# Moving one expert tile into the attention phase: units from pair 8, earlier routing, halved weight pieces, single scatter slots

## The chip, the cores and the metric

The kernel runs on one core of one Trainium2 chip. The metric is the device time of one execution in microseconds (us). Chips differ: in this study the kernel before took 203 to 210 us on two of them (12 and 4) and 221 to 226 us on two others (15 and 2). Every comparison below is a ratio to runs of the kernel before on the same chip. An execution over 1.5 per cent above the fastest of its kernel is called slow here; the ratios use the fast ones alone.

## The reference

Block-sparse attention (4 batches, 8 heads, 768 positions, head size 64) is followed by a mixture of experts in which each of the 3072 tokens goes to one of 8 experts.

```python
# attention: a window of +-15 positions, and 24 block summaries a head
k_sum = k.reshape(B, H, nb, 32, D).max(axis=3);  v_sum = v.reshape(B, H, nb, 32, D).mean(axis=3)
a = softmax([window scores | summary scores + log 32]);  x = a @ [v | v_sum]
# experts
logits = x @ w_gate + modality_bias[modality_id];  e_idx = argmax(logits, axis=1)
for e in range(8):
    mask = e_idx == e
    out[mask] = gate[mask, None] * (relu(x[mask] @ w1[e]) @ w2[e])
```

## The kernel before

Some words first. A **pair** is one of 16 attention steps (4 batches by 4 pairs of heads). After a batch's last pair its tokens are **routed** (steps on VectorE, taken by `tick`), and six indirect transfers, the **scatters**, write its rows to memory in the order of their experts. A **list** then names the tiles of 256 rows of one expert that are ready; `rows` loads them. An expert **tile** is cut into **units**: possibly a **turn** (the transposes `px` of its rows), four groups of the first product (`ph`), two of the second (`pmo`). `UNITS` says how many units run at each of six places of a pair; what attention does not take is left to the **tail**, behind attention.

```python
UNITS = {11: "111111", 12: "111111", 13: "111111", 14: "111111", 15: "101110"}   # 28 units
ENLIST = {9: 0, 12: 1, 15: 2}               # at the end of pair 9 comes batch 0's list, ...
# ...
def rows(lst, j, i):                        # cut: the last batch gathers by index instead
    row = nc.sync.value_load(lst["li"][0:1, j, 0:1], ...)
    nc.sync.dma_start(xr.bitcast(I32), xs[ds(row, 256)]...)
```

The weights of the two likeliest experts are loaded ahead, in pieces (`issue`, by the table `WAT`). Whether a tile's weight buffer really holds its expert is known only from the list. So each tile has a conditional reload of both products' weights that moves bytes only where the expert differs:

```python
def weights(lst, j, i):
    e = nc.gpsimd.value_load(li[0:1, j, 2:3], ...)
    go = nc.gpsimd.value_load(li[0:1, j, 3:4], min_val=0, max_val=1)
    load_weights(i % NWB, e, cond=go > 0)   # NWB = 2 buffers
# ...
def ahead():                                # called by enlist, by unit, and when the last piece is sent
    while todo and todo[0][2] < min(ended[0] + 1 + into[0] // 4, guessed[0]):
        lst, j, i = todo[0]; fetch(i); todo.popleft()
        weights(lst, j, i)
        pending.append(expert_tile(i))
# ...
WAT = {1: 1, 2: 1, 3: 1, 4: 2, 5: 1, 6: 2, 7: 2, 8: 2, 9: 2, 10: 2}   # quarters a pair; 8 are one expert
```

On this case's inputs no reload moves anything: the records of these instructions are 0.04 to 0.05 us long and have no packets. The loop over the pairs, cut to the places that matter (`pump` takes units, `scatter` one scatter from the queue unless told otherwise):

```python
for n in range(np_):
    scores(n, 0); ...; tick(1 if n < 10 else 2); pump(u[0]); blocks(n); ...
    scatter(early); pump(u[1]); ...; scores(n, 1); ...; scatter(early); pump(u[3])
    if n + 2 < np_: keys(n + 2); more(n + 2, (0, 1))
    ...; pump(u[4]); values(n, 0); scatter(); ...
    if n + 2 < np_: summaries(n + 2)        # GpSimd copies the block summaries into kv (line 276)
    issue(n)
    if u[3]: scatter(2)
    if n in ENLIST:
        scatter(len(scatters)); enlist(lists[ENLIST[n]])
    pump(u[5])
```

The softmax here doesn't subtract the row's maximum and nothing guards it: scores larger than these inputs give would overflow.

## Time and profile before

| | first profile | a cleaner repeat on chip 12 |
|---|---|---|
| this execution | 221.1 us | 203.9 us |
| span of the core | 219.2 us | 202.0 us |
| TensorE busy | 181.5 us | 174.6 us |
| granted clock, mean | 0.948 | 0.969 |
| timed runs | median 208.56 us (3 runs) | fast ones 203.84 and 205.82 us |

A timeline row gives start, duration, engine, line, operation, output<-input, and in brackets how long the engine had stood idle and what ended it. The first profile has 10.8 us of idle called "issue" in its second half; the repeat has none after 84 us. I use the repeat, a single execution, for comparisons. Here is its GpSimd timeline where the first reloads (line 233) and the second batch's scatters (line 372) are:

```profile
74.47 0.05 POOL L233 DMA_DIRECT2D w1b<-in_moe_w_dram  x1 [0.90 <-DMA w1b<-in_moe_w_dram]
74.92 0.04 POOL L233 DMA_DIRECT2D w2b<-in_moe_w_dram  x1 [0.40 <-DMA w2b<-in_moe_w_dram]
79.87 1.10 POOL L372 DMA_INDIRECT xs<-xb,posi  x1 [0.59 <-DVE ks L270]
...
87.95 0.04 POOL L233 DMA_DIRECT2D w2b<-in_moe_w_dram  x1 [1.42 <-DMA w2b<-in_moe_w_dram]
...
92.09 0.99 POOL L372 DMA_INDIRECT xs<-xb,posi  x1 [0.30 <-issue]
```

Tile 0's reload is met 0.9 and 0.4 us after GpSimd is free, tile 1's 1.42 us: the pieces that they must not overtake had almost all landed. The second batch's six scatters go out between 79.87 and 92.09.

### The profile page before, as it was taken

How to read it: one execution, taken by the hardware profiler on the slowest of the kernel's cores; microseconds unless marked ns; L12 is line 12 of the kernel's file. 1: busy time of each engine (PE TensorE's matmuls, PEld its weight loads, DVE VectorE, ACT ScalarE, POOL GpSimd, SP SyncE). 2: the span in 40 equal slices, each digit the busy share in tenths (PEclk: the TensorE clock that was granted, in tenths of full speed). 3: DMA queues.
4: the chain of work that ended last, by engine and by line, in shares of the span. 5: the costliest groups of instructions: out<-in, count | busy, mean ns of one | idle time of the engine just before them, and what ended most of it. 6: DMA issues, size and time to landing. Idle time of an engine off the chain costs nothing. (4 is left out here: it accounts for less than half of the span.)

```text
span 219.2 us, 7344 instructions
## 1 busy us (share of the span) xinstructions
PE 181.5 (83%) x3008; PEld 130.9 (60%) x3008; DVE 99.8 (46%) x335; ACT 129.4 (59%) x174; POOL 116.5 (53%) x189
## 2 busy tenths in 40 slices
PE   7679778798779669978999739999785999998860
PEld 2467667687669556655676524767362776676440
DVE  5378766866989993416348422353930000000000
ACT  2698779658886858757384223544433776575440
POOL 8786556556889539571303741206875337522540
PEclk9997999959979999999999966999999999999997
DMA  5999999998999999737200323203243222220220
GB/s 74 180 200 216 132 175 173 165 158 122 159 215 193 209 225 191 161 114 241 100 3 28 117 107 106 96 3 121 76 152 102 96 100 99 93 99 4 99 91 20
DMA packets 20141, 27.49 MB, mean 125 GB/s; under 512 B 2924, under 2 KB 16516, under 8 KB 20100
## 3 DMA queue, kind: packets, MB, share of 16 engines
q0 software_dynamic: 17472, 24.40, 54.1%
q1 hardware_dynamic: 2628, 2.54, 4.2%
q8 instruction: 26, 0.43, 0.8%
q14 instruction: 15, 0.12, 0.2%
HBM read 85.46 MB, written 10.17 MB: 436 GB/s over the span
## 5 line engine op out<-in xcount | busy, mean ns | idle before, releaser
L563 PE MATMUL ph<-xg,w1b 128*128 128x256 f16 x384 | 46.9, 273 | 4.2 <-issue 2.6
L575 PE MATMUL pmo<-w2b,hT 128*128 128x512 f16 x192 | 46.8, 390 | 2.7 <-issue 2.4
L563 PEld LDWEIGHTS <-w1b 128*128 128x128 f16 x384 | 35.9, 98 | 12.3 <-issue 5.8
L565 ACT ACTIVATE hT<-ph 128x512 f16<-128x512 f32 x48 | 28.5, 599 | 23.0 <-PE ph L563 17.9
L581 POOL DMA_INDIRECT out_dram<-ot,at x24 | 23.8, 992 | 31.2 <-ACT ot L579 19.6
L260 ACT COPY kv<-pk 128x1152 f16<-128x1152 f16 x32 | 34.6, 1131 | 9.3 <-PE pk L250 7.4
L317 ACT ACTIVATE pT<-pss 128x768 f16<-128x768 f32 x32 | 26.2, 820 | 10.1 <-PE pss L313 6.0
L575 PEld LDWEIGHTS <-hT 128*128 128x128 f16 x192 | 18.1, 100 | 22.7 <-issue 4.7
L372 POOL DMA_INDIRECT xs<-xb,posi x24 | 26.1, 1086 | 9.6 <-issue 6.4
L579 ACT ACTIVATE ot<-pmo,xr 128x512 f32<-128x512 f32 x24 | 16.4, 688 | 22.8 <-PE pmo L575 9.5
L549 DVE SCALAR_TENSOR_TENSOR at<-gm,xr 128x2 uint32<-128x2 f32 x13 | 2.2, 168 | 42.8 <-DMA xr<-xs,gi 42.8
L332 DVE RECIPROCAL rec<-po 128x6 f32<-128x6 f32 x32 | 6.0, 188 | 34.0 <-PE po L329 29.7
L329 PE MATMUL po<-vb,pT 120*64 120x65 f16 x384 | 13.6, 203 | 5.9 <-issue 5.9
L286 ACT COPY qT<-pq 128x768 f16<-128x768 f16 x16 | 12.9, 808 | 9.4 <-PE pq L284 6.9
L339 DVE TENSOR_TENSOR xb<-po,rec 128x384 f16<-128x384 f32 x32 | 17.8, 557 | 1.0
L296 DVE COPY vb<-pv 120x768 f16<-120x768 f16 x28 | 14.6, 553 | 6.9 <-PE pv L295 6.8
L270 DVE TENSOR_REDUCE ks<-kv 128x24 f16<-128x768 f16 x16 | 15.1, 945 | 3.6 <-ACT kv L260 3.6
L295 PE MATMUL pv<-ident,kv 128*128 128x128 f16 x192 | 15.5, 237 | 0.3 <-issue 0.3
L329 PEld LDWEIGHTS <-pT 120*64 120x64 f16 x384 | 10.4, 118 | 8.0 <-issue 7.6
L276 POOL COPY kv<-ks 128x576 f16<-128x576 f16 x16 | 10.8, 678 | 7.9 <-DVE ks L275 4.1
L295 PEld LDWEIGHTS <-kv 128*128 128x128 f16 x192 | 13.1, 107 | 1.7 <-issue 0.6
L313 PE MATMUL pss<-qT,kv 64*128 64x64 f16 x384 | 11.8, 195 | 2.4 <-POOL kv L276 1.4
(142 smaller groups left out, 283.4 us busy)
## 6 DMA issues: line engine op xcount, KB each, us to landing
w1b<-in_moe_w_dram POOLq DMA_DIRECT2D x13, 1024.0 KB
w2b<-in_moe_w_dram POOLq DMA_DIRECT2D x13, 1024.0 KB
kn<-in_k_dram POOLq DMA_DIRECT2D x16, 192.0 KB
vn<-in_v_dram POOLq DMA_DIRECT2D x16, 192.0 KB
qn<-in_q_dram POOLq DMA_DIRECT2D x16, 192.0 KB
xr<-xs SPq DMA_DIRECT2D x8, 272.0 KB, 4.9
w1b<-in_moe_w_dram POOLq DMA_DIRECT2D x8, 256.0 KB
w2b<-in_moe_w_dram POOLq DMA_DIRECT2D x8, 256.0 KB
```

The lines of the kernel that those rows point to most:

```text
L260: nc.scalar.copy(kv[:, i, :, 0:WK].rearrange("p t (s c) -> p t s c", c=C8), bass.AP(pb.tensor, pb.offset, [pb.ap[0], [8, NT], [1, 12], [P8 ...
L270: nc.vector.reduce_max(ks[:, 0], kv[:, 0, :, 16:80].rearrange("p t (g s) -> p t g s", g=2), axis=AX.X)
L295: nc.tensor.transpose(pv[:, tl, :], kv[:, 1, 6 * half + tl, :], ident)
L317: nc.scalar.activation(pT.rearrange("p h t s -> p h (t s)"), two, AF.Exp, scale=SCALE)
L329: nc.tensor.matmul(po[64 * (tl % 2):64 * (tl % 2) + 64, h, tl // 2, :], pT[0:KR, h, tl, :], vb[0:KR, 6 * half + tl, h, :])
L339: nc.vector.tensor_tensor(xo, po[:, :, :, 0:D], rec.unsqueeze(3).to_broadcast([128, 2, 3, D]), op=ALU.mult)
L372: apart("xs", nc.gpsimd.indirect_dma_start(out=xs[:, :], out_offset=bass.IndirectOffsetOnAxis(ap=posi[:, j:j + 1], axis=0), in_=xb[:, c, : ...
L563: nc.tensor.matmul(ph[:, f, :], w1[:, c, ts(2 * f2 + f, 128)], xg[:, c, :], start=(c == 0), stop=(c == NCD - 1))
L565: nc.scalar.activation(hT[:, 2 * f2:2 * f2 + 2, :], ph, AF.Relu)
L575: nc.tensor.matmul(po, hT[:, f, ts(s2, 128)], w2[:, f, :], start=(f == 0), stop=(f == NF - 1))
L579: nc.scalar.activation(ot, po, AF.Copy, scale=gt)
L581: apart("out", nc.gpsimd.indirect_dma_start(out=out[:, :], out_offset=bass.IndirectOffsetOnAxis(ap=at[:, s2:s2 + 1], axis=0), in_=ot[:], i ...
```

## The change

The intent: TensorE has gaps in attention and is full in the tail, so take one more tile (35 units rather than 28) out of the tail and start it three pairs earlier. To have its rows by then, route two steps at a time from pair 5 and spread the scatters over five single slots a pair. To have its weights, send the second expert's in halves and be done a pair earlier. The V sums go to VectorE from pair 9, and GpSimd's drain (`nc.gpsimd.drain()`, one call in the tail) comes a tile earlier.

```diff
-    NSUM = 12
+    TWO = 5
+    NSUM = 9
-    UNITS = {11: "111111", 12: "111111", 13: "111111", 14: "111111", 15: "101110"}
-    ENLIST = {9: 0, 12: 1, 15: 2}
+    UNITS = {8: "000111", 9: "011011", 10: "001110", 11: "011100", 12: "111111", 13: "111111", 14: "111111", 15: "101110"}
+    ENLIST = {7: 0, 11: 1, 14: 2}
-    WAT = {1: 1, 2: 1, 3: 1, 4: 2, 5: 1, 6: 2, 7: 2, 8: 2, 9: 2, 10: 2}
+    WAT = {1: 1, 2: 1, 3: 1, 4: 1, 5: 1, 6: 1, 7: 2, 8: 2, 9: 2}
     def issue(n):
         for _ in range(WAT.get(n, 0)):
             p = sent[0]
-            sent[0] += 1
+            two = p >= 8
+            sent[0] += 1 + two
... (parts of a half of w1b or w2b instead of a quarter; two assertions that the weights were sent)
-        tick(1 if n < 10 else 2)
+        tick(1 if n < TWO else 2)
... (the same at every tick of the loop)
         pump(u[4])
+        scatter(early)
         values(n, 0)
... 
-        if u[3]:
-            scatter(2)
+        scatter()
...
     while ended[0] < last:
+        if ended[0] == last - 3:
+            nc.gpsimd.drain()
         if ended[0] == last - 2:
             ...
-            nc.gpsimd.drain()
```

More of the change, by code (lines that the diff above doesn't have):

```diff
@@ L224, in later_constants, with load_weights @@
         nc.vector.tensor_tensor(base, base, mb0[:, 0:1, :].to_broadcast([128, NJ, E]), op=ALU.add)
-    def load_weights(u, e, which=(0, 1), part=None, **kw):
+    def load_weights(u, e, which=(0, 1), part=None, parts=1, **kw):
         for i in which:
@@ L230, in load_weights @@
             if part is not None:
-                n = dst.shape[1] // 4
+                n = dst.shape[1] // parts
                 src, dst = src[:, ts(part, n)], dst[:, ts(part, n)]
@@ L558, in expert_tile @@
         hT = work.tile([128, NF, 256], FP16, tag="hT", bufs=2, name="hT")
+        assert sent[0] >= min(8 * i + 4, 16)
         for f2 in range(NF // 2):
@@ L572, in expert_tile @@
                 turn(i + 1)
+            assert sent[0] >= min(8 * i + 8, 16)
             po = bank([128, DM], FP32, "pmo")
@@ L685, in issue @@
             p = sent[0]
-            sent[0] += 1
+            two = p >= 8
+            sent[0] += 1 + two
             if p % 8 == 0:
                 gv[p // 8] = nc.gpsimd.value_load(guess[0:1, p // 8:p // 8 + 1], min_val=0, max_val=E - 1)
-            load_weights(p // 8, gv[p // 8], which=(p // 4 % 2,), part=p % 4)
-            if p == 7:
+            load_weights(p // 8, gv[p // 8], which=(p // 4 % 2,), part=p % 4 // (1 + two), parts=4 // (1 + two))
+            if sent[0] == 8:
                 guessed[0] = 1
-            if p == 15:
+            if sent[0] == 16:
                 guessed[0] = NTILE + NWB
@@ L710 @@
             features(n - 2)
-        tick(1 if n < 10 else 2)
+        tick(1 if n < TWO else 2)
         pump(u[0])
         blocks(n)
-        tick(1 if n < 10 else 2)
+        tick(1 if n < TWO else 2)
         early = n - 1 not in ENLIST
@@ L729 @@
             logits(b - 1)
-        tick(1 if n < 10 else 2)
+        tick(1 if n < TWO else 2)
         pump(u[2])
         scores(n, 1)
-        tick(1 if n < 10 else 2)
+        tick(1 if n < TWO else 2)
         scatter(early)
@@ L738 @@
             more(n + 2, (0, 1))
-        tick(1 if n < 10 else 2)
+        tick(1 if n < TWO else 2)
         pump(u[4])
+        scatter(early)
         values(n, 0)
         scatter()
-        tick(1 if n < 10 else 2)
-        tick(1 if n < 10 else 2)
+        tick(1 if n < TWO else 2)
+        tick(1 if n < TWO else 2)
         if n + 2 < np_:
@@ L747 @@
         issue(n)
-        tick(1 if n < 10 else 2)
-        if u[3]:
-            scatter(2)
+        tick(1 if n < TWO else 2)
+        scatter()
         if n in ENLIST:
```

## The prediction

> **What bounds the kernel now.** I read the page's totals and slices first, then the timelines of TensorE, GpSimd and VectorE, then the waits. No engine is full over the whole span, so the stages have to be told apart:
>
> ```profile
> PE 181.5 (83%) x3008; PEld 130.9 (60%) x3008; DVE 99.8 (46%) x335; ACT 129.4 (59%) x174; POOL 116.5 (53%) x189
> PE   7679778798779669978999739999785999998860
> POOL 8786556556889539571303741206875337522540
> DMA  5999999998999999737200323203243222220220
> ```
>
> To be seen: GpSimd and the DMA engines are loaded in the first half (attention, its loads, the early weights), TensorE in the second. In TensorE's timeline pair 8 starts at 58.03 us, pair 9 at 63.82, 10 at 69.84, 11 at 75.26, 12 at 88.31; attention ends near 143.5. The first expert tile begins here:
>
> ```profile
> 65.56 1.05 POOL L372 DMA_INDIRECT xs<-xb,posi  x1 [0.30 <-DMA kn<-in_k_dram]
> 70.39 0.40 SPq L521 DMA_DIRECT2D xr<-xs  x1
> ```
> ```profile
> 74.10 0.18 PE L445 MATMUL pc<-tot,ones 128*128 128x8 f16 x1 [1.15 <-DVE tot L441]
> 78.08 0.62 PE L544 MATMUL px<-ident,xr 128*128 128x128 f16 x8 [1.86 <-DMA xr<-xs]
> ```
>
> To be seen: the last of the six row scatters of batch 0 is issued at 65.56; the load of the sorted rows starts when it has landed (70.39) and lands at 78.0. TensorE waited 1.86 us for it. So **12.5 us** lie between the last scatter and the first expert matmul, and the rows are already the later of the two. The tail is the other stage:
>
> ```profile
> 163.48 1.05 POOL L523 DMA_INDIRECT xr<-xs,gi  x1 [0.40 <-issue]
> 164.83 1.01 POOL L523 DMA_INDIRECT xr<-xs,gi  x1 [0.30 <-issue]
> ```
> ```profile
> 165.26 2.33 PE L575 MATMUL pmo<-w2b,hT 128*128 128x512 f16 x10 [1.41 <-issue]
> 169.26 3.65 PE L563 MATMUL ph<-xg,w1b 128*128 128x256 f16 x32 [1.67 <-issue]
> 174.48 0.61 PE L544 MATMUL px<-ident,xr 128*128 128x128 f16 x8
> ```
>
> To be seen: tile 8, the first that needs the last batch's routing, gathers its rows at 163.48 and 164.83; by the trace's semaphore records they land at 167.4. TensorE asks for them at 174.48, so they don't bind. A full tile costs TensorE **7.39 us** (first matmuls at 176.65, 184.04, 191.44). The idle times called "issue" in the second half (1.8 us at 96 to 99, 0.5 at 109, 4.4 at 126 to 130, 1.0 at 155, then 1.4 and 1.7) sum to some 10.8 us. The profiled run took 221.1 us against 208.6 timed, so I choose to read them as a cost of profiling.
>
> **What the Trainium skill says.** "DMA: Bandwidth & Descriptors", section on the anatomy of one software DMA, gives a fixed cost of about 2 us per transfer, most of it the receipt of the write. The trace agrees where the DMA engines are free (scatters at 118 to 128 us land after 2.3 us), but under load the scatters of 54 to 66 us take 4.4 to 5.4, and row loads range from 2.9 to 9.2. "Runtime: NRT & Kernel Launch", section on instruction fetch mechanics, says instructions stream in 16 KiB blocks, mostly hidden; the page's 26 packets on the instruction queue fit, and TensorE's idle of about 1 us every 5 us before 55 us fits fetches that the loads delay. "TensorE: Matmul & The Clock Gate", Part 1, says that an idle array falls to half its clock; the trace has granted-clock dips of that kind, one near 65 to 68 us, during attention. "Perfetto Trace Analysis", section on the most-contended engine, warns that matmul busy time is no measure of headroom; so I use start-to-start times.
>
> **The change part by part.** Units in a timeline: four matmul groups of the first product at 0.97 us, two of the second at 1.73, one turn of the rows at 0.45.
>
> 1. Units in attention: 28 become 35, one whole tile with its turn, so the tail has one tile less: minus 7.39 us there, plus 7.39 us of TensorE work in pairs 8 to 11.
>
> 2. What those pairs can absorb. From pair 8's middle (60.7) to pair 12 (88.31) the kernel now takes 27.6 us. It holds 6.5 us of expert units (a turn, four groups, one second-product group, a turn). The new schedule holds 15.6 there (pair 8: a turn and two groups, 2.4; 9: two groups, two of the second product, a turn, 5.85; 10: three groups, 2.9; 11: one and two, 4.4). The other 21.1 us hold about 14 of attention at full clock; the rest is 1.1 (idle at 62), 1.15 (count sum), 2.3 (rows and their copy), some 1.7 lost to the half clock, and small gaps. If all of it fills up, the stretch takes 14.0 + 15.6 = 29.6 us plus perhaps 2 of gaps and a late pair 8, against 27.6: attention ends **4.0 us later**.
>
> 3. Block sums of V leave TensorE for three pairs: 16 small matmuls, about 0.28 us a pair start to start, so 0.85 us saved (already in the 29.6). VectorE gets 0.94 for 0.17 us, 2.3 us in all, mostly beside TensorE work.
>
> 4. Tail: the route chain does not shrink with the tail. Logits at 146.7 to rows landed at 167.4 is some 20 us: VectorE 4 us to the positions, then GpSimd for six scatters at 1.3 us, two output scatters and the gathers. TensorE's slack before tile 8 is 174.5 - 167.4 = 7.1 us, of which 4.05 (0.97 + 1.41 + 1.67) is idle that I put down to profiling. Some 3 us remain, and the change takes 7.39 out of them: TensorE then **waits about 4.3 us** at tile 8. Parts 1 to 4: 4.0 - 7.39 + 4.3 = +0.9 us.
>
> 5. Rows of tile 0. Routing two steps at a time from pair 5 makes the positions ready at that pair's end, and the five slots a pair bring the sixth scatter to the end of pair 6, behind one weight piece. GpSimd is late there: it ends pair 5's work at 48.5, then has five scatters at 1.37 us with their gap (6.9), three loads (1.9), the copy (0.8) and a piece (0.7) before the sixth: about 59 to 60 us, only 6 us earlier than now. The first turn, however, moves from 76.2 to about 62, 14 us earlier. From scatter to landing I take 4.5 + 6.5 = 11 us (12.5 now): rows at some 70 to 71, a **wait of 8 us, at best 3.5** with unloaded latencies (2.3 + 2.9).
>
> 6. First weights: pieces 7 and 8 come with pair 7, the rest in halves in pairs 8 and 9; by GpSimd's order they land before use. The GpSimd drain a tile earlier: that engine stands 5.9 us before 199.54, and TensorE then loses about 1.5 us. The gather of the tile before has some 3 us of slack, so I expect the cost to move, not to vanish: 0, give or take 1.
>
> **Rivals.** (a) Rows in time: the routing and slots are matched to pair 8, which speaks for a schedule tuned on a chip. Then only +0.9 us remains, or down to -5 if the second-half idle is real (no wait at tile 8) and the clock stays up. (b) Rows late, as reckoned in 5: +4 to +10 us, because TensorE runs in order and attention behind the turn stands too. GpSimd at 8 to 9 tenths at 50 to 70 us and the present wait of 1.86 speak for it. (c) The tail turns into a wait on the route chain, so a saved tile is worth only 3 us; the list of the slack speaks for it. (d) Contention: halves of weights in pairs 8 and 9 delay rows and fetches by 1 to 2 us; the loads of 70 to 74 us already take 8 to 10 us to land.
>
> **Range and chances.** The working alone gives 0.9 + 8 = +8.9 us (217.5). Against it stands that schedules this particular are seldom written without a measurement; I weight (b) a little over half. The middle is **212 us**, the range **203.5 to 220**. Chances: faster 0.16, within 2% 0.42, slower 0.42.
>
> **What would show it.** Right: TensorE idle of 4 us or more before the first transposes of the sorted rows in pair 8, released by their load; the sixth scatter of batch 0 after 58 us; pairs 9 to 11 without idle; attention ending later, not at the same time; an idle of 3 to 5 us before tile 8's transposes, released by the gather. Wrong: the rows landing before TensorE comes (scatters earlier, or attention slower, than I reckon), a tail shorter by a full 7.4 us, or second-half idle that stays as large in timed runs.

## The result, and the profile after

The changed kernel took **234.69 us** (median of 4 runs, 233.79 to 235.27), the kernel before 207.9 us (207.24 to 208.95, 4 runs). The ratio of the fast runs is **1.128** (95% interval 1.121 to 1.135): slower. A ratio here is the mean time of one kernel's fast runs over that of the other's fast runs of the same rounds, so it is not quite the ratio of the medians quoted. The profiled execution was 233.79 us.

From the page of the changed kernel, the totals, the slices and the groups of two kinds of matmuls with the idle time ahead of them (last column):

```profile
PE 187.0 (81%) x2960; PEld 135.8 (59%) x2960; DVE 101.4 (44%) x335; ACT 130.2 (56%) x174; POOL 114.1 (49%) x185
PE   7799995985708996993279999999999299968970
POOL 8666664568923433078700311673177735147231
PEclk9956997999555999799558999999999979999997
L545 PE MATMUL px<-ident,xr 128*128 128x128 f16 x104 | 9.4, 237 | 18.6 <-DMA xr<-xs 13.3
L314 PE MATMUL pss<-qT,kv 64*128 64x64 f16 x384 | 12.6, 201 | 10.8 <-POOL kv L277 7.7
```

TensorE has fewer matmuls but is busy 187.0 us, 12.4 more than in the clean repeat of before, and idle 44.8 us (231.8 less 187.0) against 27.4. So of the 29.8 us between the two spans, 17.4 are idle and 12.4 are slower matmuls. The clock row shows why those are slower: fives at slices 11 to 13 and 20 to 21, where TensorE had stood. Not all of it is the change's: 3.6 of the 12.4 us come in the first 58 us (busy 48.2 against 44.6), before the clock fell behind any wait listed below; there it was at half from 10.7 to 20.9 us, before the schedules part. Most of the idle is in two groups, 18.6 us ahead of the transposes of sorted rows and 10.8 us ahead of the attention scores; in the first profile of before the score group had 2.4 us.

TensorE's long waits in its timeline after:

```profile
58.92 0.50 PE L314 MATMUL pss<-qT,kv 64*128 64x64 f16 x12 [2.96 <-POOL kv L277]
70.52 1.03 PE L545 MATMUL px<-ident,xr 128*128 128x128 f16 x8 [7.19 <-DMA xr<-xs]
91.46 1.05 PE L565 MATMUL ph<-xg,w1b 128*128 128x256 f16 x8 [2.24 <-DMA w1b<-in_moe_w_dram]
...
105.81 0.34 PE L308 MATMUL pss<-ident,bterm 64*128 64x384 f16 x2
110.22 0.50 PE L314 MATMUL pss<-qT,kv 64*128 64x64 f16 x12 [4.07 <-POOL kv L277]
117.55 1.03 PE L545 MATMUL px<-ident,xr 128*128 128x128 f16 x8 [6.07 <-DMA xr<-xs]
...
129.75 0.34 PE L308 MATMUL pss<-ident,bterm 64*128 64x384 f16 x2
...
183.21 0.23 PE L545 MATMUL px<-ident,xr 128*128 128x128 f16 x1 [3.37 <-DMA xr<-xs,gi]
184.55 0.77 PE L545 MATMUL px<-ident,xr 128*128 128x128 f16 x7 [1.12 <-DMA xr<-xs,gi]
```

In order: the copy of summaries on GpSimd, tile 0's rows, tile 1's first weights, the copy again, tile 2's rows (the second batch's first), and in the tail tile 8's gathered rows. The two rows without a wait are the first scores of pairs 12 and 13, so the 4.07 and 6.07 us both stand in pair 12. And GpSimd's timeline at the same places:

```profile
59.88 1.04 POOL L373 DMA_INDIRECT xs<-xb,posi  x1 [0.30 <-issue]
...
63.58 1.54 POOL L234 DMA_DIRECT2D w2b<-in_moe_w_dram  x2
72.92 0.04 POOL L234 DMA_DIRECT2D w2b<-in_moe_w_dram  x1 [7.80 <-issue]
...
89.16 1.51 POOL L234 DMA_DIRECT2D w2b<-in_moe_w_dram  x2
91.40 0.04 POOL L234 DMA_DIRECT2D w1b<-in_moe_w_dram  x1 [0.73 <-DMA w1b<-in_moe_w_dram]
97.31 0.04 POOL L234 DMA_DIRECT2D w2b<-in_moe_w_dram  x1 [5.86 <-DMA w2b<-in_moe_w_dram]
98.28 1.07 POOL L373 DMA_INDIRECT xs<-xb,posi  x1 [0.93 <-issue]
...
110.34 1.00 POOL L373 DMA_INDIRECT xs<-xb,posi  x1 [0.17 <-issue]
```

The sixth scatter of batch 0 goes at 59.88. The last two weight pieces of tile 0 are issued at 63.58; its conditional reload stands right behind them, and by the trace's semaphore records the second piece lands at 72.7: GpSimd stands **7.80 us** for a reload that moves nothing. The same happens for tile 1 (halves issued at 89.16, landed at 97.3, **5.86 us**). VectorE had the second batch's positions at 86.04; their first scatter goes at 98.28, once the reload is past.

The reload holds TensorE directly too. By the semaphore records the pieces of tile 1's first weights had landed at 88.18, but TensorE's 2.24 us end at 91.46, just behind the w1b reload of 91.40 that moves nothing. Other runs have the same pair of times: in e9 (below) the reload at 97.86 and TensorE at 97.92, in e11 102.18 and 102.33, where the pieces had landed at 86.18.

The second batch's positions were themselves late. They came 13.2 us later than in the repeat of before, because the routing stands in program order behind pair 8, in which TensorE waited (in e3 below, without that wait, they come at 73.47 us):

```profile
72.81 0.20 DVE L429 TENSOR_REDUCE posi<-rk 128x6 uint32<-128x48 f32 x1
```
```profile
86.04 0.20 DVE L430 TENSOR_REDUCE posi<-rk 128x6 uint32<-128x48 f32 x1
```

### The profile page after: what moved, and what is told of

The parts are those of the page before. It is cut to its first block, busy times and chain, and to the rows that moved or that the text cites. A ratio compares the mean times of both kernels' runs of the same rounds, so it can differ in the third digit from the quotient of the medians.

```text
span 231.8 us, 7231 instructions
## 1 busy us (share of the span) xinstructions
PE 187.0 (81%) x2960; PEld 135.8 (59%) x2960; DVE 101.4 (44%) x335; ACT 130.2 (56%) x174; POOL 114.1 (49%) x185
## 5 line engine op out<-in xcount | busy, mean ns | idle before, releaser
L565 PE MATMUL ph<-xg,w1b 128*128 128x256 f16 x384 | 49.8, 284 | 4.2 <-DMA w1b<-in_moe_w_dram 4.2
L578 PE MATMUL pmo<-w2b,hT 128*128 128x512 f16 x192 | 46.1, 388 | 0.0
L565 PEld LDWEIGHTS <-w1b 128*128 128x128 f16 x384 | 37.2, 101 | 11.5 <-DMA w1b<-in_moe_w_dram 3.9
L373 POOL DMA_INDIRECT xs<-xb,posi x24 | 24.8, 1034 | 9.2 <-issue 8.6
L545 PE MATMUL px<-ident,xr 128*128 128x128 f16 x104 | 9.4, 237 | 18.6 <-DMA xr<-xs 13.3
L314 PE MATMUL pss<-qT,kv 64*128 64x64 f16 x384 | 12.6, 201 | 10.8 <-POOL kv L277 7.7
L314 PEld LDWEIGHTS <-kv 64*128 64x128 f16 x384 | 11.0, 102 | 14.0 <-POOL kv L277 8.4
L545 PEld LDWEIGHTS <-xr 128*128 128x128 f16 x104 | 7.0, 105 | 20.1 <-DMA xr<-xs 13.7
L277 POOL COPY kv<-ks 128x576 f16<-128x576 f16 x16 | 10.8, 675 | 14.3 <-DVE ks L276 11.0
L547 ACT COPY xg<-px 128x1024 f16<-128x1024 f16 x10 | 10.1, 1010 | 13.3 <-PE px L545 13.3
```

The source lines that it names most:

```text
L314: nc.tensor.matmul(pss[h][:, tl, :], kv[rr, 0, t, :], qT[rr, ts(t, 8), :].rearrange("p s c -> p (s c)"), start=False, stop=True, skip_grou ...
L373: apart("xs", nc.gpsimd.indirect_dma_start(out=xs[:, :], out_offset=bass.IndirectOffsetOnAxis(ap=posi[:, j:j + 1], axis=0), in_=xb[:, c, : ...
L545: nc.tensor.transpose(px[:, c, s2, :], xr[:, s2, ts(c, 128)], ident)
L565: nc.tensor.matmul(ph[:, f, :], w1[:, c, ts(2 * f2 + f, 128)], xg[:, c, :], start=(c == 0), stop=(c == NCD - 1))
L578: nc.tensor.matmul(po, hT[:, f, ts(s2, 128)], w2[:, f, :], start=(f == 0), stop=(f == NF - 1))
```

## The experiments

All kernels gave correct results. Where the two reloads are left out the kernel is right for these inputs only, and meant as an experiment. The theory: (A) tile 0 starts before its rows, (B) the reloads of tiles 0 and 1 hold GpSimd, (C) the rival to B: the scatter slots and GpSimd's backlog alone make the second batch late, (D) the larger weight pieces crowd the DMA engines, (E) the early routing itself costs.

### First four: what binds

**before_again**: the kernel before, unchanged, one look.

> The kernel before, unchanged, to get a second trace. Theory: the first trace's 'issue' idle on TensorE (some 11 us from 96 us on) came from that one execution, which took 221 us against 208 timed; a run of about 208 us should show under 2 us of such idle after 96 us. Rival: the idle is in every run, and a trace of 208 us still shows 8 us or more of it.

Measured on chip 12: 203.87 us, the clean profile used above.

**e1_drain_back**: the changed kernel with the drain where it was.

```diff
-        if ended[0] == last - 3:
-            nc.gpsimd.drain()
         if ended[0] == last - 2:
+            nc.gpsimd.drain()
```

> The changed kernel with GpSimd's drain put back behind tile 9. Theory A: the drain's cost only moves; in the changed kernel TensorE waits 1.9 us for the weight check and 0.9 us for rows after it, before it lost about 1.6 us at the same kind of place; so 0 to -2 us, about 233.5. Rival: the earlier drain is a cause of the loss, -3 us or more.

Measured on chip 12: 230.74 us (229.97 to 232.23), ratio 1.128 (1.109 to 1.146), equal to the changed kernel's. The gap of 1.94 us ahead of the weights in the tail is gone from the trace, but no gain can be seen in the ratio, whose interval would hide one of that size.

**e2_no_check01**: the changed kernel without the reloads of tiles 0 and 1.

```diff
-            weights(lst, j, i)
+            if i >= NWB:
+                weights(lst, j, i)
```

> The changed kernel without the conditional weight reloads of tiles 0 and 1 (on these inputs their condition is false, so the result stays right; in general it would not). Theory B: these reloads hold GpSimd's in-order queue until the speculative weights have landed (7.8 us at 65 to 73, 5.9 us at 91 to 97), and by that the scatters of batch 1 come some 6 us late. Then the first of those scatters goes at about 92 instead of 98, the waits before tile 2 (4.1 us for the sums' copy, 6.1 us for rows) fall below 3 us together, and the time falls by 9 to 13 us. Rival C: the slots themselves bind the scatters; then at most -3 us.

Measured on chip 12: 225.34 us (224.16 to 225.88), ratio 1.098 (1.083 to 1.113). From its GpSimd timeline, then its TensorE timeline:

```profile
90.64 1.07 POOL L373 DMA_INDIRECT xs<-xb,posi  x1 [0.30 <-issue]
...
103.37 1.00 POOL L373 DMA_INDIRECT xs<-xb,posi  x1 [0.17 <-issue]
```
```profile
110.26 1.03 PE L545 MATMUL px<-ident,xr 128*128 128x128 f16 x8 [6.23 <-DMA xr<-xs]
```

The first scatter of the second batch comes 7.6 us earlier and the waits for the copy (4.07 us) and for tile 1's weights (2.24 us) vanish, so B holds; yet tile 2's rows are as late for TensorE as in the changed kernel (6.23 us), so C is half right too: what the reloads gave back, the next wait took in part. The gain forecast, 9 to 13 us, was missed: by the ratios it is 3.0 points, some 6 us, and the waits before tile 2 did not fall below 3 us.

**e3_pair_later**: the same 35 units, but from pair 9 on.

```diff
-    UNITS = {8: "000111", 9: "011011", 10: "001110", 11: "011100", 12: "111111", ...
+    UNITS = {9: "000111", 10: "011011", 11: "111111", 12: "111111", ...
```

> The changed kernel with the 13 expert units of pairs 8 to 11 put into pairs 9 to 11 (3, 4, 6), nothing else changed. Theory D: the wait of 7.2 us for the rows of tile 0, and the half clock after it (about 3 us), come from starting before the rows can be there; one pair later the wait is under 2 us and the time falls by 6 to 10 us. Rival: TensorE's work is what counts, the wait moves elsewhere, and the time changes by less than 2 us.

Measured on chip 12: 225.26 us (223.42 to 225.94), ratio 1.097 (1.078 to 1.116). From its GpSimd and its TensorE timeline:

```profile
93.90 0.04 POOL L234 DMA_DIRECT2D w2b<-in_moe_w_dram  x1 [7.39 <-DMA w2b<-in_moe_w_dram]
95.61 1.02 POOL L373 DMA_INDIRECT xs<-xb,posi  x1 [0.30 <-issue]
```
```profile
69.32 0.62 PE L545 MATMUL px<-ident,xr 128*128 128x128 f16 x8 [0.72 <-DMA xr<-xs]
107.28 1.03 PE L545 MATMUL px<-ident,xr 128*128 128x128 f16 x8 [11.12 <-DMA xr<-xs]
```

Tile 0's wait is gone (0.72 us), which shows A. But TensorE now comes to tile 2 sooner, and tile 1's reload falls between the second and the third scatter of the second batch (7.39 us): the wait there grows to 11.12 us. The time fell by 3.1 points, some 6 us, the low edge of the forecast.

### Both causes, and parts alone, on a slow chip

**after_again**: the changed kernel once more.

> The changed kernel unchanged, as the control for the runs of this call and for the drain experiment. Expected: 1.12 to 1.14 times the kernel before, and the same TensorE idle before tile 0 (7 us), tile 2 (6 us) and tile 8 (4.5 us). If the idle wanders by more than 1 us from run to run, the readings of single traces are weaker than I treat them.

Measured on chip 15: 246.79 us (244.59 to 247.47), before 223.95 us, ratio 1.107 (1.097 to 1.118), with 8.45 us at tile 0, 4.15 at the copy and 5.81 at tile 2. As a control it half failed: the ratio is below the 1.12 to 1.14 expected, tile 0's wait differs from the first trace's 7.19 by more than the 1 us allowed, and tile 8's 4.5 us are absent (the tail has idle called "issue" instead). Waits of single traces are therefore good to a microsecond or so, and across chips less.

**e5_later_nocheck**: the edits of e2 and e3 together.

> Both edits together: expert units of pairs 8 to 11 in pairs 9 to 11, and no conditional reloads for tiles 0 and 1 (right on these inputs only). In the run with the later pair alone, the check of tile 1 held GpSimd from 86.5 to 93.9 us, between the second and third scatter of batch 1, and TensorE waited 11.1 us before tile 2. Theory B (the check holds the scatters): that wait falls below 5 us, and the time to about 216 to 219, 1.05 to 1.06 times before. Rival C (slots and a late pair bind): the wait stays above 8 us and the time above 222.

Measured on chip 15: 223.58 us (221.58 to 224.25), ratio 0.999 (0.988 to 1.010). I took this to mean that the two causes are the whole loss. It was wrong, as e5_again below shows.

**e6_before_route**: the kernel before with only the routing from pair 5 and the five single slots.

> The kernel before with only the earlier routing (two steps at a time from pair 5) and the five single slots of the change; units, weights and lists as before. Theory E: five scatters in pair 6 (6.9 us of GpSimd) push the sums' copy behind them, TensorE waits some 3 us for it before pair 8, and the time rises by 1 to 4 us. Rival: that wait is hidden by the slack of the pairs without experts, and the time stays within 1 us.

Measured on chip 15: 233.15 us (231.93 to 235.41), ratio 1.049 (1.036 to 1.061). No clean test of E: the list stayed at pair 9, so the second batch's six scatters (75.85 to 82.43 us) came into the queue ahead of the list, and the load of tile 0's rows waited for them as well; 8.88 us of TensorE's idle stand before the first transposes. It shows that a row load of this program waits for scatters emitted ahead of it, its own batch's or not: by the semaphore records the last of the second batch's landed at 85.37 us, and the load of tile 0's rows was issued at 85.38.

**v1_start10**: as e6, with the list a pair earlier and three units in pair 10 (31 units).

```diff
-    UNITS = {11: "111111", 12: ...        -    ENLIST = {9: 0, 12: 1, 15: 2}
+    UNITS = {10: "000111", 11: "111111", 12: ...   +    ENLIST = {8: 0, 11: 1, 14: 2}
```

> A version meant to beat both: the kernel before with the earlier routing and slots, lists after pairs 8, 11 and 14, and three expert units in the second half of pair 10, where the rows of tile 0 (landing near 70.5 us in the changed kernel) are already there; weights, sums and drain as before. If the waits for rows are what spoils the change, this has none above 1 us before tiles 0 and 2, and takes 1 to 4 us less than before. Rival: the tail is bound by the route chain of the last batch (slack 4 us before tile 8 in the clean trace), GpSimd's load makes new waits, and it gains nothing.

Measured on chip 15: 219.7 us (218.0 to 220.59), ratio **0.984** (0.972 to 0.995). So with the list moved along, routing, slots and three units more are together a small gain; E falls as a main cause. What routing and slots cost by themselves, net of the three units, was not measured.

### Four with five rounds: the small parts

**v1_again**: v1_start10 on another chip.

> The kernel before with routing two pieces at a time from pair 5, five single scatter slots a pair and the first unit in pair 10. Theory (rows of tile 0 and of tile 2 decide): the first turn comes after the rows have landed, no wait over 1 us before the transposes of tiles 0 and 2, one half tile moved forward for nothing lost: ratio 0.97 to 0.995, as in its first run (0.984). Rival (the first run was a chance of its chip): ratio 0.995 to 1.01.

Measured on chip 4: 203.29 us (202.85 to 206.16), before 206.08 us, ratio **0.991** (0.984 to 0.997): a small gain, seen on two chips. Tile 8's rows land at 157.4 us and TensorE asks at 157.8: the tail's slack is used up to 0.4 us. Tile 2's rows cost 2.18 us.

**e4_before_drain3**: the kernel before with the drain a tile earlier.

> The kernel before with GpSimd's drain one tile earlier, nothing else. Theory (the earlier drain costs the 2 us that the trace of the undone drain showed at the next tile's first weights): 1 to 2.5 us slower, ratio 1.005 to 1.012, with TensorE idle of about 2 us before the first product of the tile after the drain. Rival (the cost only moves, as the prediction had it): ratio 0.996 to 1.004, one gap of 0.8 to 2 us gone where the drain was and one of the same size where it is now.

Measured on chip 4: 206.39 us (205.11 to 208.69), ratio 1.005 (0.998 to 1.013). Between my theory (1.005 to 1.012) and its rival (0.996 to 1.004), undecided; with e1 (no difference) the medians put the drain's place at about 1 us or less, while the interval reaches 2.7 us (1.3 per cent).

**e8_nocheck_drain_back**: e5 with the drain back.

> The changed kernel with the units one pair later, without the conditional reloads of tiles 0 and 1, and with the drain back in its old place. Theory (the three causes add): the gap of some 1.6 us at the drain's place goes, ratio to before 0.985 to 0.995 where the version with the drain moved had 0.999. Rival (the gather of the last tiles ends later then and takes it back): ratio 0.996 to 1.01. It leaves out a reload that other inputs would need, so it is an experiment only.

Measured on chip 4: 212.82 us (211.13 to 217.03), ratio 1.037 (1.029 to 1.045). A plain miss: neither 0.99 nor the rival's at most 1.01. Something of 3.5 per cent was still in it, so the sum "rows plus reloads" did not hold.

**v1n9**: v1_again with the V sums on VectorE from pair 9 (`NSUM = 9`).

> As v1_again, with the block sums of V on VectorE from pair 9 on rather than from pair 12. The prediction's part 3: TensorE loses 16 small matmuls a pair over three pairs, 0.85 us, VectorE gains 2.3 us beside other work: ratio to before 0.003 to 0.005 below that of v1_again. Rival (VectorE feeds the routing in these pairs, so its 2.3 us come back as a later wait): the same ratio or up to 0.005 higher.

Measured on chip 4: 203.73 us (202.45 to 204.58), ratio 0.993 (0.987 to 1.000), inside v1_again's interval. The 0.85 us that I had reckoned for it cannot be seen.

### Six more: dividing the loss

**e5_again**: the same kernel as e5.

> The version with units one pair later and without the conditional reloads of tiles 0 and 1, that had a ratio of 0.999 on a chip where the kernel before took 224 us. Since then the same with the drain in its old place had 1.037 on a chip where the kernel before took 206 us. Theory (the ratio of 0.999 belongs to that slow chip, whose own idle time struck the kernel before harder; rows and reloads explain only two thirds of the loss, and the rows of tile 8 most of the rest): on a chip where before takes 203 to 210 us this takes 212 to 216 us, ratio 1.03 to 1.05, with some 4 to 5.5 us of TensorE idle before tile 8's transposes and 2 to 4 before tile 0's. Rival (putting the drain back cost time): ratio 0.99 to 1.01.

Measured on chip 12: 216.31 us (212.53 to 218.9; four of the seven runs were slow, the fast ones took 212.53 to 213.54), before 206.0 us, ratio 1.035 (1.026 to 1.044). The 0.999 belonged to the slow chip. Its profile fell in the slow state (one look, clock 0.922), so only the order of its TensorE waits is read:

```profile
72.16 0.91 PE L545 MATMUL px<-ident,xr 128*128 128x128 f16 x8 [1.80 <-DMA xr<-xs]
99.54 0.98 PE L545 MATMUL px<-ident,xr 128*128 128x128 f16 x8 [2.61 <-DMA xr<-xs]
167.44 0.23 PE L545 MATMUL px<-ident,xr 128*128 128x128 f16 x1 [4.29 <-DMA xr<-xs,gi]
```

The largest wait left is at tile 8, in the tail. The fast profile of e8 has it as 4.17 and 1.20 us.

**e9_half_tile**: the changed kernel with 31 units, from pair 10, and nothing else altered.

```diff
-    UNITS = {8: "000111", 9: "011011", 10: "001110", 11: "011100", 12: "111111", ...
+    UNITS = {10: "000111", 11: "111111", 12: "111111", ...
```

> The changed kernel with one alteration: the first unit in pair 10, then full pairs, so 31 units in attention where the changed kernel has 35 and the kernel before 28. Theory (what is lost is lost because tile 0 starts before its rows, tile 2 before its rows and the tail runs out of slack; all three come from starting a tile early, not from the routing, the slots or the halves): idle under 1.5 us before the transposes of tile 0 and of tile 8, under 3 us before tile 2's, ratio 0.985 to 1.005 (the drain's half per cent is still in it). Rival (the conditional reloads hold GpSimd wherever the tile starts): GpSimd idle of 5 us or more among the second batch's scatters, TensorE idle of 5 us or more before tile 2, ratio 1.02 to 1.05.

Measured on chip 12: 214.11 us (212.7 to 215.55), ratio 1.040 (1.033 to 1.047). The rival won: waits for rows are gone at tiles 0, 2 and 8 (none above 0.5 us ahead of their transposes), but GpSimd stands 8.85 us for tile 0's reload, and the attention scores wait for its copy. The rival had placed the hold among the second batch's scatters and TensorE's wait before tile 2; it came ahead of them, and the wait at the scores of pair 10. From its GpSimd and TensorE timelines:

```profile
64.14 1.54 POOL L234 DMA_DIRECT2D w2b<-in_moe_w_dram  x2
74.53 0.04 POOL L234 DMA_DIRECT2D w2b<-in_moe_w_dram  x1 [8.85 <-issue]
```
```profile
77.91 0.50 PE L314 MATMUL pss<-qT,kv 64*128 64x64 f16 x12 [6.44 <-POOL kv L277]
```

**e10_half_tile_nocheck**: e9 without the reloads of tiles 0 and 1.

> As the run before, also without the conditional reloads of tiles 0 and 1, which other inputs would need. Theory of the start: the same time within 1 us. Rival (the reloads hold GpSimd wherever the tile starts): 5 us or more faster than the run before, ratio 0.985 to 1.0.

Measured on chip 12: 206.02 us (205.03 to 209.51), ratio 1.002 (0.995 to 1.008): 8 us below e9, and level with the kernel before. The idle of 6.44 us before the scores is gone, and so is e9's wait of 2.43 us at tile 1's first weights. Two reloads that move no byte cost 3.8 per cent.

**e11_quarters**: the changed kernel with quarters on before's table `WAT`.

> The changed kernel with the first weights in quarters on the schedule of the kernel before, nothing else. Theory (the conditional reload of tile 1 holds GpSimd until the last piece has landed; quarters are issued until pair 10, later than the halves): that hold is as long or longer, ratio to before 1.12 to 1.16. Rival (the larger pieces of 512 KB crowd the DMA engines and delay rows): rows of tile 2 earlier, 1 to 3 us faster than the changed kernel, ratio 1.11 to 1.12.

Measured on chip 12: 229.44 us (226.58 to 230.49), ratio 1.108 (1.097 to 1.119). My number (1.12 to 1.16) missed; the rival's (1.11 to 1.12) is met at its edge, but not for its reason, since tile 2's rows came no earlier (117.95 us against 117.55). With the old table the eighth quarter comes in pair 6, and GpSimd does not stand at tile 0's reload (0.04 us, at 65.36); at tile 1's it stands 4.73 us. The waits moved: 9.76 us for tile 0's rows, 7.93 for tile 1's first weights (ended by their empty reload, as said above), 3.46 for tile 2's rows. Whether larger pieces crowd the DMA engines (D) stays open.

**e12_list8**: e9 with batch 0's list one pair later; every reload stays.

```diff
-    ENLIST = {7: 0, 11: 1, 14: 2}
+    ENLIST = {8: 0, 11: 1, 14: 2}
```

> The changed kernel with its first unit in pair 10 (31 units, ratio 1.040) and the first row list one pair later, at the end of pair 8, so that tile 0's conditional reload of the weights comes into GpSimd's queue a pair after the weight pieces instead of right behind them. All reloads stay. Theory (the reload's place is what costs 8 us, not that it exists): GpSimd's hold of 8.85 us at 74.5 us shrinks to under 3 us, the idle of 6.4 us before the scores of pair 9 goes, ratio 0.995 to 1.015. Rival (the second tile's reload takes the first one's place): holds of 5 us or more later, ratio 1.02 to 1.04.

Measured on chip 2, a slow one: 224.03 us (222.75 to 228.48), before 222.57 us, ratio 1.004 (0.998 to 1.010). Ratios ran lower on slow chips (e5: 0.999 against 1.035). The GpSimd timeline:

```profile
68.59 1.44 POOL L234 DMA_DIRECT2D w1b<-in_moe_w_dram  x2 [0.61 <-issue]
70.77 0.05 POOL L234 DMA_DIRECT2D w1b<-in_moe_w_dram  x1 [0.74 <-DMA w1b<-in_moe_w_dram]
71.45 0.04 POOL L234 DMA_DIRECT2D w2b<-in_moe_w_dram  x1 [0.64 <-DMA w2b<-in_moe_w_dram]
```

The same two conditional reloads now cost 0.74 and 0.64 us, and in this run no attention score waits for the copy of summaries. What costs is the reload's place, a few instructions behind the pieces that it must not overtake. The ratio on a fast chip was not measured.

**v1_full_tile**: v1_again with a whole tile more than before, 35 units from pair 9.

```diff
-    UNITS = {10: "000111", 11: "111111", ...
+    UNITS = {9: "000111", 10: "011011", 11: "111111", ...
```

> The version v1_again (31 units, ratio 0.991, rows of tile 8 landed only 0.4 us before TensorE asks for them) with four units more, from pair 9 on: a whole tile more in attention than before, as in the change, but with quarters of weights, the list at pair 8 and the old drain. Theory (a tile taken from the tail is worth nothing beyond the slack of the route chain): TensorE waits 4 to 6 us before tile 8's transposes, and the rows of tile 0 are 2 to 4 us late; 4 to 9 us slower than v1_again, ratio 1.01 to 1.035. Rival (only the reloads and the first rows were at fault): no more than 2 us of idle at tile 8, ratio 0.98 to 1.0.

Measured on chip 2: 235.23 us (232.81 to 236.93), ratio 1.053 (1.047 to 1.059). More than either side expected; v1 itself had 0.984 on the other slow chip. The profile fell in the slow state, so again only the kinds of waits are read: 4.84 us for tile 0's rows, 2.86 for tile 1's weights, 5.02 for tile 2's rows, 4.21 and 1.07 for tile 8's. Even with the old weights, the old drain and the late list, a whole tile brings back all the waits of the changed kernel except the copy's.

### What the runs say together

The six kernels that share everything else form a table of ratios to before. Five were run on chip 12; the change itself was not, and its 1.128 comes from the chip of the result (with the drain back, e1, it was 1.128 on chip 12):

| units in attention | reloads of tiles 0 and 1 in | left out |
|---|---|---|
| 35, from pair 8 (the change) | 1.128 | 1.098 |
| 35, from pair 9 | 1.097 | 1.035 |
| 31, from pair 10 | 1.040 | 1.002 |

The reloads cost 3.0, 6.2 and 3.8 points, and the early start with its four units more 9.6 points without reloads (1.098 against 1.002): 6.3 for pair 8 instead of 9, 3.3 for the four units more. The intervals are 0.7 to 1.9 points to either side. The two are not simply additive. A reason that fits, not tested alone: at pair 8 GpSimd's first hold lies largely in the time in which TensorE waits for tile 0's rows anyway. The version v1_again, which has routing, slots and three units more but the old weights and drain, beats the kernel before by about 1 per cent. e10, without two reloads, stayed level with before; which of halves, drain, V sums and earlier list makes that last point, if it is one (the intervals touch), was not separated.

## Why the prediction was wrong

The prediction was 212 us, within 203.5 to 220; 234.69 were measured. The trace lets the error be placed. Logits of the last batch come at 164.06 us in the changed kernel and at 133.67 in the clean one of before: attention ends **30.4 us later**. From there to the end the core takes 67.7 us against 68.3: the tail is 0.6 us shorter.

- **Part 1, one tile less in the tail: right**, and worth nothing. Full tiles still follow each other at 7.39 us (191.85 to 199.24 us).
- **Part 4, the route chain: right.** Predicted 20 us from logits to rows and a wait of 4.3 us at tile 8; measured 20.5 us (164.06 to 184.55) and 3.37 + 1.12 = 4.5 us. Tail by parts 1 and 4 was -3.1 us, measured -0.6; the other 2.5 us include the 1.94 us gap at the next weights, which e1 shows to be the drain's.
- **Part 5, tile 0's rows: right.** Sixth scatter predicted at 59 to 60 us, measured at 59.88; wait predicted at 8 us, measured at 7.19. The working holds too: scatter to landing was reckoned at 4.5 + 6.5 us, and the semaphore records give 3.8 + 6.8. e3 removes the wait by starting later. So rival (b) came true in its mechanism, and (c) with it; (a) fell. That the "issue" idle of the first profile is a cost of profiling, as I chose to read it, is not shown, and probably wrong. After 96 us the twelve profiles on chips 12 and 4 have none of it, the six on chips 15 and 2 have 4.7 to 10.6 us. The first profile's 11 us and its time of 221.1 us are those of a slow chip; the record does not say which it had. What makes the slow chips idle is open.
- **Part 2, attention ends 4.0 us later: the step that failed.** With part 5's wait it should have been 12 us. By the first scores of each pair, pair 8 starts at 55.62 us in the changed kernel (57.52 in the repeat of before), pair 12 at 105.81 (87.30), pair 13 at 129.75 (98.47), pair 15 at 152.87 (122.03). So the stretch that I reckoned, pairs 8 to 11, takes 20.4 us longer where 12 were predicted: the waits for the copy (2.96 us) and at tile 1's first weights (2.24) and the half clock were not in it. The wait of 2.96 is not the change's alone: the kernel before with only its drain moved (e4) had 2.55 us of it. Pair 12, where my reckoning stopped, takes 12.8 us longer, with 4.07 us of wait for the copy and 6.07 for tile 2's rows. Tile 2 is the second batch's first. It now stands in pair 12 rather than 13, but by the clock TensorE asks for it later than before (111.5 us against 99.3), and its rows land later still (117.5 against 98.0). The arithmetic of scatter times that I did for batch 0 was not done for batch 1: positions 13.2 us later behind tile 0's wait, then 12.2 us to the first scatter (7.1 before), of which 5.86 are the reload of part 6.
- **Part 6, "by GpSimd's order they land before use": failed.** I counted what GpSimd issues, not what it waits for. The reload of each tile waits in that queue for the pieces ahead of it: 7.80 and 5.86 us; and TensorE waits for the reload, 2.24 us at tile 1. e2, e9 against e10, and e12 show it. The drain's "0, give or take 1" stood (e1, e4).
- **A cost that no part charged:** the low clock behind the waits; part 2 counted only some 1.7 us of it, in the kernel before (where I read the dip at 65 to 68 us; the record has 63.4 to 66.8). After the waits of 2.24 us and more TensorE ran at half clock for stretches of 3.4 us and multiples, in one case 17.1 us (58.5 to 75.5). In the stretch from 58 to 76 us it was busy 9.9 us at a mean granted clock of 0.53. At most 8.8 of the 12.4 us of slower matmuls can be the waits' doing, since 3.6 lie in the first 58 us; the split by wait was not tried.
- **Rival (d), crowding:** the last six pieces took 5.4 to 8.4 us to land in the changed kernel, the longest a quarter (8.4) and not a half (5.4 to 8.0), but no run separates their size from their time; open. **Part 3**, the V sums, is too small to be seen (v1n9).
- **The middle of the range: the wrong discount.** The working gave 217.5 and I lowered it to 212 because such schedules "are seldom written without a measurement". No view of the profile stood behind that; without it the working would still have been 17 us short.

What stays open: why chips 15 and 2 are 17 us slower with idle called "issue", and how the 9.6 points of the early start divide among the rows of tiles 0, 2 and 8 and the low clock.

## What to carry to other kernels

Moving work ahead moves every consumer behind it ahead in program order as well, and a wait at the first one delays what produces the data of the next: for each one, and not only for the first, set the time at which it will ask beside the time at which its data lands. In this kernel a conditional transfer that was never taken still stood in its queue until the buffer's earlier writes had landed, so it belongs a stage behind those writes. And work taken from a stage behind a serial chain gains only the slack of that chain: here 3.8 us (in the clean trace of before, tile 8's rows land at 153.5 us and are asked for at 157.3), used up to 0.4 us by half a tile (v1_again).

## What the Trainium skill lacked or had wrong

- "DMA: Bandwidth & Descriptors", the section on the anatomy of one software DMA, says that waits on semaphores happen on the issuing sequencer before dispatch. The runs agree and add what it lacks: a conditional transfer whose condition is false waits there too, 7.80 and 5.86 us here. Its fit, 2.0 us and the bytes over 436e3 a microsecond, gives 3.2 us as an estimate for a half of 512 KB; under this kernel's load tile 1's halves took 5.4 to 8.0 us.
- "TensorE: Matmul & The Clock Gate", Part 1, gives a free-running window of 3413 ns; the trace agrees (low-clock stretches of 3.4, 6.8, 10.2, 13.7 and 17.1 us). The long stretch ended as the page says, after a busy window: cut into windows of 3.4 us from 58.5 us on, TensorE was busy 2.96, 1.44, 0.00, 1.61 us and then throughout, and full clock came back. The stretch of 10.7 to 20.9 us does not fit: by the trace, whose matmul ends are modelled, TensorE was busy through all three of its windows. What the page lacks is how idle a window must be: half clock followed windows with 0.88 us (55.1 to 58.5) and 1.17 us (89.2 to 92.6) of busy TensorE, the latter with a single wait of 2.24 us.
- No page has the difference between chips: the same kernel took 206 us on two and 223 us on two others, which turned one ratio from 1.035 to 0.999.
- No page says what an explicit drain of GpSimd costs. The engine stood 6.3 us before the instruction behind it in the changed kernel, and moving it changed the time of the kernel before by 0.5 per cent (interval -0.2 to 1.3, so no change is shown).
